# Attention and bilinear FFN on one core: a written order on all engines, six-token loads for batches 0 and 1, and later q transposed by DMA

## The chip, the cores and the metric

One core of a Trainium2 chip runs the whole program in one launch. The metric is the device time of one execution in microseconds; lower is better.

## The reference

Eight batches, eight heads, 576 tokens, head size 64; all inputs are float32. The result has 4608 tokens of 512 values.

```python
kv  = einsum('bhsd,bhse->bhde', k, v)                 # per head 64 x 64, sum over 576 tokens
out = einsum('bhsd,bhde->bhse', q, kv)
x   = out / sqrt(mean(out*out, axis=-1) + 1e-6) * g_norm   # then heads side by side: 4608 x 512
a, b = x @ w_a, x @ w_b                               # 512 -> 1536 each
y   = (a * b) @ w_out                                 # 1536 -> 512
```

## The kernel before

**Attention of one batch** (class `Attn`) goes by head pairs p = 0 to 3, two heads to 128 partitions. `kv(p)` sums over the 576 tokens in five chunks (four of 128 tokens, one of 64) with k as the weights, and ScalarE copies the two diagonal blocks to `kvd` (lines 146 to 162). `qT(p)` transposes q by five TensorE transposes into PSUM, and VectorE copies it to `qs` (164 to 176). `xu(p, h)` multiplies by `kvd` for half of the tokens (288) and ScalarE squares the result; `ss(p, h)` sums the squares by a matmul with a constant matrix, ScalarE takes the reciprocal root, VectorE scales into `xt[p]` (178 to 205). `slices()` yields after each of these pieces: 17 pieces to a batch.

**Loads** (`load_b`, lines 73 to 94) are DMAs from the GpSimd queue that cast float32 to bfloat16. A partition holds four consecutive tokens of a head, a run of 1024 bytes in DRAM and 512 bytes in SBUF; the last 64 tokens go in a second DMA in runs of 256 and 128 bytes. Since TensorE wants the two heads of a pair side by side, VectorE copies k and q into another order first (`reorder`, 125 to 130). The token order inside a batch is thus permuted, and `store` (246 to 264) writes rows with a stride of four to undo it.

**FFN** goes by nine strips of 512 tokens. `ffn_ab(s, fc)` is one of twelve units of a strip: four matmuls with `w_a`, four with `w_b`, each of 512 columns; ScalarE copies the first result, VectorE multiplies the second by it. `ffn_o(s, g)` is twelve matmuls for 128 tokens, a copy and one or two stores from the SP queue.

**Order.** Loads are issued as batch 0, `w_a` and `w_b` in twelve DMAs, batch 1, `w_out` in two, batch 2, then one batch per strip. The program is written as: attention 0, the units of strip 0, attention 1, then strips 1 to 8, where each unit of strip s is followed by a piece of the attention of batch s+1, and every third unit by an `ffn_o` of strip s-1. A planner of the tile framework reorders the instructions within each engine's queue by what it estimates to be ready; `kr` copies of batch 2 can so stand ahead of VectorE work of strip 0. Each engine then runs its queue in order.

Of the kernel before, what the change touches and what calls it, by code (L numbers as in the profile page):

```python
# [8 lines left out]
FP32 = mybir.dt.float32  # L9
# [6 lines left out]
def kernel(  # L16
# [20 lines left out]
    NCH = S // 128  # L37
    SA = NCH * 128
    SB = S - SA
# [24 lines left out]
    def load_ab(i):  # L64
        sl = slice(i * WCH, (i + 1) * WCH)
        nc.gpsimd.dma_start(out=wa_t[:, :, sl], in_=wa_v[:, :, sl])  # L66
        nc.gpsimd.dma_start(out=wb_t[:, :, sl], in_=wb_v[:, :, sl])  # L67

    def load_o(i, n):
        sl = slice(i * n, (i + 1) * n)  # L70
        nc.gpsimd.dma_start(out=wo_t[:, sl, :], in_=wo_v[:, sl, :])

    def load_b(b, parts):
        tiles = {}
        for name in ("k", "v", "q"):
            tiles[name] = qkv_pool.tile([128, H, NCH + 1, D], BF16, name=name + "t", tag=name)
            if name != "v":
                tiles[name + "r"] = qkv_pool.tile(
                    [128, NCH + 1, H, D], BF16, name=name + "r", tag=name + "r", bufs=2
                )  # L80
        hn = H // parts
        for i in range(parts):
            hs = slice(i * hn, (i + 1) * hn)
            for name, src in (("k", k), ("v", v), ("q", q)):
                t = tiles[name]
                nc.gpsimd.dma_start(  # L86
                    out=t[:, hs, 0:NCH, :],
                    in_=src[b, hs, 0:SA, :].rearrange("h (sp c) d -> sp h c d", c=NCH),
                )
# [12 lines left out]
    g_col = const.tile([128, 1], FP32)
    g_src = g_norm.rearrange("(d u) -> d u", u=1)
    nc.sync.dma_start(out=g_col[0:D, :], in_=g_src)
    nc.sync.dma_start(out=g_col[D : 2 * D, :], in_=g_src)
    eps_t = const.tile([128, 1], FP32)
    nc.vector.memset(eps_t, EPS)
    warm = const.tile([128, 1], FP32)
    nc.scalar.activation(warm, eps_t, AF.Abs_reciprocal_sqrt)
    ones = const.tile([128, 128], BF16)  # L110
# [3 lines left out]
    kvd = []  # L114
    for i in range(2):
        t = const.tile([128, NP, 128], BF16, name=f"kvd{i}")
        nc.vector.memset(t, 0.0)
        kvd.append(t)

    xt = []  # L120
    for kc in range(KC):
        xt.append(xt_pool.tile([128, n_tok], BF16, name=f"xt{kc}", tag=f"xt{kc}"))


    def reorder(t, name, hs):
        nc.vector.tensor_copy(
            t[name + "r"][:, 0:NCH, hs, :],
            t[name][:, hs, 0:NCH, :].rearrange("p h c d -> p c h d"),
        )
        nc.vector.tensor_copy(t[name + "r"][0:SB, NCH, hs, :], t[name][0:SB, hs, NCH, :])  # L130

    class Attn:
        def __init__(self, b, t, parts):
            self.b, self.t, self.parts = b, t, parts
            self.kvd = kvd[b % 2]
            self.qs = {}
            self.kv_ps = None
            self.x_ps = {}
            self.sq = {}

        def need(self, name, p):
            n = NP // self.parts
            if p % n == 0:
                reorder(self.t, name, slice(2 * p, 2 * p + 2 * n))

        def kv(self, p):
            if p == 0:
                self.kv_ps = apsum.tile([128, NP, 128], FP32, name="kv_ps", tag="at")
            kt, vt = self.t["kr"], self.t["v"]
            hs = slice(2 * p, 2 * p + 2)  # L150
            self.need("k", p)
            for c in range(NCH + 1):
                r = 128 if c < NCH else SB
                nc.tensor.matmul(  # L154
                    self.kv_ps[:, p, :],
                    lhsT=kt[0:r, c, hs, :],
                    rhs=vt[0:r, hs, c, :],
                    start=(c == 0),
                    stop=(c == NCH),
                )  # L160
            nc.scalar.copy(self.kvd[0:D, p, 0:D], self.kv_ps[0:D, p, 0:D])
            nc.scalar.copy(self.kvd[D:, p, D:], self.kv_ps[D:, p, D:])

        def qT(self, p):
            qt = self.t["qr"]
            hs = slice(2 * p, 2 * p + 2)
            self.need("q", p)
            ps = apsum.tile([128, S], BF16, name="q_ps", tag="at")
            for c in range(NCH + 1):
                r = 128 if c < NCH else SB  # L170
                nc.tensor.transpose(  # L171
                    ps[:, c * 128 : c * 128 + r], qt[0:r, c, hs, :], ident[0:r, 0:r]
                )
            qs = asb_pool.tile([128, S], BF16, name="qs", tag="qs", bufs=5)
            nc.vector.tensor_copy(qs, ps)
            self.qs[p] = qs

        def xu(self, p, h):
            ps = apsum.tile([128, HF], FP32, name="x_ps", tag="at")
            nc.tensor.matmul(  # L180
                ps,
                lhsT=self.kvd[:, p, :],
                rhs=self.qs[p][:, h * HF : (h + 1) * HF],
                start=True,
                stop=True,
            )
            sq = asb_pool.tile([128, HF], BF16, name="sq", tag="sq")
            nc.scalar.activation(sq, ps, AF.Square)  # L188
            self.x_ps[p, h] = ps
            self.sq[p, h] = sq  # L190

        def ss(self, p, h):
            ps = apsum.tile([128, HF], FP32, name="s_ps", tag="at")
            nc.tensor.matmul(ps, lhsT=ones, rhs=self.sq[p, h], start=True, stop=True)  # L194
            rs = asb_pool.tile([128, HF], FP32, name="rs", tag="rs")
            nc.scalar.activation(rs, ps, AF.Abs_reciprocal_sqrt, bias=eps_t)  # L196
            t0 = self.b * S + h * HF
            nc.vector.scalar_tensor_tensor(  # L198
                out=xt[p][:, t0 : t0 + HF],
                in0=self.x_ps[p, h],  # L200
                scalar=g_col,
                in1=rs,
                op0=ALU.mult,
                op1=ALU.mult,
            )

        def slices(self):
            for p in range(NP):
                self.kv(p)
                yield  # L210
                self.qT(p)
                yield
            prev = None
            for p in range(NP):
                for h in range(2):
                    self.xu(p, h)
                    if prev is not None:
                        self.ss(*prev)
                    prev = (p, h)
                    yield  # L220
            self.ss(*prev)
            yield


    ab = {}

    def ffn_ab(s, fc):
        t0 = s * STRIP
        a_ps = fpsum.tile([128, STRIP], FP32, name="a_ps", tag="f")
        b_ps = fpsum.tile([128, STRIP], FP32, name="b_ps", tag="f")  # L230
        for w, ps in ((wa_t, a_ps), (wb_t, b_ps)):
# [117 lines left out]
```

## Time and profile before

| | |
|---|---|
| time, two runs | 369.06 and 369.86 us, median 369.46 us |
| span of the profiled execution | 369.4 us (the profile gives no other time of its own) |
| TensorE busy | 341.7 us, 93% of the span, 1744 matmuls |
| VectorE, ScalarE busy | 149.7 us, 140.2 us |
| GpSimd queue's DMAs | 45,728 packets, 18.88 MB written |
| SP queue's DMAs | 5,664 packets, 9.44 MB written |

Busy time of TensorE is modelled and pipelined, so a busy engine is not one at its peak: the distance between the starts of consecutive matmuls says more. The table's 93% is a mean over a start, in which data is loaded, and a long regular part; the stretches are to be read one by one. MB and GB/s of the loads count the bfloat16 bytes written; the float32 bytes read are twice as many.

### The profile page before, as it was taken

The page shows a single profiled execution, that of the slowest core. Times are in us where ns is not written, and L with a number is a line of the kernel's source. Part 1 is how long each engine was busy: PE and PEld are TensorE (multiplying, and loading weights), DVE is VectorE, ACT ScalarE, POOL GpSimd, SP SyncE. Part 2 cuts the span into 40 slices and gives each one's busy share as a digit, 9 for nine tenths or more (in the row PEclk, how much of TensorE's full clock was granted, in tenths as well). Part 3 has the DMA queues.
Part 4 walks back from the last instruction along what each step waited for, and adds up shares of the span by engine and source line. Part 5 has one row for each costly group of instructions (what it writes and reads, how often), then busy time and mean ns, then how long its engine had stood idle before and what let it go on. Part 6 is the DMA issues. An engine that isn't in the chain of part 4 may idle for free.

```text
span 369.4 us, 4627 instructions
## 1 busy us (share of the span) xinstructions
PE 341.7 (93%) x1744; PEld 163.8 (44%) x1744; DVE 149.7 (41%) x268; ACT 140.2 (38%) x320; POOL 57.6 (16%) x80
## 2 busy tenths in 40 slices
PE   0588859999999999999999999999999999999994
PEld 0333324444444444445444444444444444444441
DVE  1343535545543554355434543354335432222310
ACT  1164113633562356235523552355235522132210
POOL 7955635535000200020000000000000000000000
PEclk9999885699999999999999999999999999999998
DMA  8999999999901511151001111100001111101023
GB/s 96 177 196 192 165 193 192 191 191 204 210 32 30 69 51 31 29 73 49 28 30 28 28 30 29 30 28 29 30 28 30 28 28 30 29 28 59 28 58 85
DMA packets 51414, 28.61 MB, mean 77 GB/s; under 512 B 14528, under 2 KB 46784, under 8 KB 51392
## 3 DMA queue, kind: packets, MB, share of 16 engines
q0 software_dynamic: 45728, 18.88, 41.5%
q1 hardware_dynamic: 5664, 9.44, 9.2%
q8 instruction: 13, 0.21, 0.3%
q14 instruction: 9, 0.07, 0.1%
HBM read 37.75 MB, written 9.44 MB: 128 GB/s over the span
## 4 chain that ended last, share of the span: by engine, by line
PE 81%; DMA 11%; POOL 3%; ACT 2%; DVE 1%; issue 1%; POOLq 0%; ACTq 0%; DVEq 0%
PE o_ps L269 26%; PE a_ps L233 23%; PE b_ps L233 22%; DMA kt<-in_k_dram 4%; PE kv_ps L154 3%; PE q_ps L171 3%; DMA wa_t<-in_moe_w_a_dram 3%; DMA qt<-in_q_dram 2%; PE s_ps L194 2%; DMA vt<-in_v_dram 2%; PE x_ps L180 2%; POOL wb_t L67 1%; POOL wa_t L66 1%; ACT rs L196 1%; ACT sq L188 0%
## 5 line engine op out<-in xcount | busy, mean ns | idle before, releaser
L243 DVE TENSOR_TENSOR abt<-b_ps,a_sb 128x512 bf16<-128x512 f32 x108 | 74.4, 691 | 100.7 <-PE b_ps L233 94.2
L241 ACT CAST a_sb<-a_ps 128x512 bf16<-128x512 f32 x108 | 63.1, 586 | 108.1 <-PE a_ps L233 106.5
L269 PE MATMUL o_ps<-wo_t,abt 128*128 128x512 bf16 x432 | 98.6, 379 | 0.0
L233 PEld LDWEIGHTS <-wb_t 128*128 128x128 bf16 x432 | 42.8, 99 | 60.6 <-issue 13.3
L269 PEld LDWEIGHTS <-abt 128*128 128x128 bf16 x432 | 41.3, 98 | 46.7
L233 PEld LDWEIGHTS <-wa_t 128*128 128x128 bf16 x432 | 39.9, 99 | 39.0 <-issue 2.4
L233 PE MATMUL b_ps<-xt_122,wb_t 128*128 128x512 bf16 x108 | 42.4, 393 | 6.4 <-DVE abt L243 6.4
L233 PE MATMUL a_ps<-xt_122,wa_t 128*128 128x512 bf16 x108 | 42.6, 394 | 0.0
L233 PE MATMUL a_ps<-xt_123,wa_t 128*128 128x512 bf16 x108 | 41.9, 388 | 0.0
L233 PE MATMUL a_ps<-xt_125,wa_t 128*128 128x512 bf16 x108 | 41.2, 381 | 0.7 <-DVE xt_125 L198 0.5
L233 PE MATMUL b_ps<-xt_123,wb_t 128*128 128x512 bf16 x108 | 41.8, 387 | 0.0
L233 PE MATMUL b_ps<-xt_125,wb_t 128*128 128x512 bf16 x108 | 41.4, 384 | 0.0
L233 PE MATMUL b_ps<-xt_124,wb_t 128*128 128x512 bf16 x108 | 41.4, 384 | 0.0
L233 PE MATMUL a_ps<-xt_124,wa_t 128*128 128x512 bf16 x108 | 41.2, 381 | 0.2 <-DVE xt_124 L198 0.2
L188 ACT ACTIVATE sq<-x_ps 128x288 bf16<-128x288 f32 x64 | 26.1, 411 | 33.2 <-PE x_ps L180 32.8
L196 ACT ACTIVATE rs<-s_ps,eps_t 128x288 f32<-128x288 f32 x64 | 31.7, 498 | 1.9 <-PE s_ps L194 1.7
L154 PE MATMUL kv_ps<-vt,kr 128*128 128x128 bf16 (+1 forms) x160 | 20.2, 241 | 13.0 <-DMA vt<-in_v_dram 12.0
L280 DVE COPY o_sb<-o_ps 128x512 f32<-128x512 f32 x18 | 12.5, 692 | 38.3 <-PE o_ps L269 38.3
L278 ACT COPY o_sb<-o_ps 128x512 f32<-128x512 f32 x18 | 10.5, 586 | 45.4 <-PE o_ps L269 45.4
L154 PEld LDWEIGHTS <-kr 128*128 128x128 bf16 (+1 forms) x160 | 13.9, 105 | 24.4 <-issue 6.9
L86 POOL DMA_DIRECT2D vt<-in_v_dram x10 | 9.4, 941 | 77.1 <-PE kv_ps L154 71.6
L194 PE MATMUL s_ps<-sq,ones 128*128 128x288 bf16 x64 | 19.7, 308 | 1.8 <-ACT rs L196 0.7
(42 smaller groups left out, 196.4 us busy)
## 6 DMA issues: line engine op xcount, KB each, us to landing
out_dram<-o_sb SPq DMA_DIRECT2D x40, 128.0 KB, 2.4
out_dram<-o_sb SPq DMA_DIRECT2D x16, 256.0 KB, 2.2
kt<-in_k_dram POOLq DMA_DIRECT2D x6, 512.0 KB, 12.6
vt<-in_v_dram POOLq DMA_DIRECT2D x6, 512.0 KB, 10.7
qt<-in_q_dram POOLq DMA_DIRECT2D x6, 512.0 KB, 12.4
wa_t<-in_moe_w_a_dram POOLq DMA_DIRECT2D x6, 256.0 KB, 8.4
wb_t<-in_moe_w_b_dram POOLq DMA_DIRECT2D x6, 256.0 KB, 9.0
wo_t<-in_moe_w_out_dram POOLq DMA_DIRECT2D x2, 768.0 KB, 9.7
```

Source lines behind the costliest of these rows:

```text
L86: nc.gpsimd.dma_start(out=t[:, hs, 0:NCH, :], in_=src[b, hs, 0:SA, :].rearrange("h (sp c) d -> sp h c d", c=NCH),)
L154: nc.tensor.matmul(self.kv_ps[:, p, :], lhsT=kt[0:r, c, hs, :], rhs=vt[0:r, hs, c, :], start=(c == 0), stop=(c == NCH),)
L171: nc.tensor.transpose(ps[:, c * 128 : c * 128 + r], qt[0:r, c, hs, :], ident[0:r, 0:r])
L188: nc.scalar.activation(sq, ps, AF.Square)
L194: nc.tensor.matmul(ps, lhsT=ones, rhs=self.sq[p, h], start=True, stop=True)
L196: nc.scalar.activation(rs, ps, AF.Abs_reciprocal_sqrt, bias=eps_t)
L233: nc.tensor.matmul(ps, lhsT=w[:, kc, fc * 128 : (fc + 1) * 128], rhs=xt[kc][:, t0 : t0 + STRIP], start=(kc == 0), stop=(kc == KC - 1),)
L241: nc.scalar.copy(a_sb, a_ps)
L243: nc.vector.tensor_mul(t, b_ps, a_sb)
L269: nc.tensor.matmul(o_ps, lhsT=ab[s, fc][:, g * 128 : (g + 1) * 128], rhs=wo_t[:, fc, :], start=(fc == 0), stop=(fc == FC - 1),)
L278: nc.scalar.copy(o_sb, o_ps)
L280: nc.vector.tensor_copy(o_sb, o_ps)
```

## The change

The tile framework's planner is switched off (`manual_schedule`), and every engine runs its instructions as written. PSUM banks and SBUF buffers are assigned by hand. For batches 0 and 1 a partition holds six consecutive tokens of a head (96 partitions, runs of 1536 and 768 bytes), loaded by head pair; k, v and q are used where they lie, one head at a time with 64 columns, and the permuted token order is kept until the stores. For batches 2 to 7 k and v come in natural token order in ten DMAs (runs of 256 and 128 bytes), q goes to a DRAM scratch as bfloat16 with the heads side by side and from there through one transposing DMA on the SP queue into `qT`. The VectorE reorder copies are gone, and for batches 2 to 7 the TensorE transposes with them. For batches 0 and 1 the square, the root and the scaling take 576 columns at once. Matmuls on zeros (`dummy`) are added to batch 0. The four `ffn_o` of strip 0 are moved from strip 1 to between the pieces of attention 1. The last `ffn_o` is stored in two halves.

```diff
-    def reorder(t, name, hs):
...
+    ctx.enter_context(tc.manual_schedule())
+    def load_early(b, p, names="kvq"):
+        hs = slice(2 * p, 2 * p + 2)
+        for n, t, src in (("k", ek, k), ("v", ev, v), ("q", eq, q)):
+            if n in names:
+                nc.gpsimd.dma_start(
+                    out=t[b][:, hs, :, :],
+                    in_=src[b, hs].rearrange("h (t c) d -> t h c d", c=EC),
                 )
...
+    def load_late(b):
+        nc.gpsimd.dma_start(
+            out=qs_d[b - 2].rearrange("t (h d) -> h t d", d=D), in_=q[b]
+        )
+        for t, src in ((lk, k), (lv, v)):
+            for c in range(NCH):
                 nc.gpsimd.dma_start(
+                    out=t[b % 3][:, c, :, :],
+                    in_=src[b, :, c * 128 : (c + 1) * 128, :].rearrange("h p d -> p h d"),
                 )
+            nc.gpsimd.dma_start(
+                out=t[b % 3][0:SB, NCH, :, :],
+                in_=src[b, :, SA:S, :].rearrange("h p d -> p h d"),
+            )
+    def transpose_q(b):
+        nc.sync.dma_start_transpose(qT[b % 2], qs_d[b - 2])
...
+            if self.early:
+                for c in range(EC):
+                    for j in range(2):
+                        r = slice(j * D, (j + 1) * D)
+                        nc.tensor.matmul(
+                            o[r, r],
+                            lhsT=ek[self.b][:, 2 * p + j, c, :],
+                            rhs=ev[self.b][:, 2 * p + j, c, :],
...
+        def qt(self, p, bank):
+            for c in range(EC):
+                for j in range(2):
+                    nc.tensor.transpose(
+                        t[j * D : (j + 1) * D, c, :],
+                        eq[self.b][:, 2 * p + j, c, :],
+                        ident[0:EP, 0:EP],
+                    )
+            nc.vector.tensor_copy(qT[self.b % 2][:, p, :], bank.bitcast(BF16)[:, 0:S])
...
+        def x2(self, p, i0):
+            for h in range(2):
+                nc.tensor.matmul(
+                    P[:, i0 + h, 0:HF],
+                    lhsT=self.kvd[:, p, :],
+                    rhs=qT[self.b % 2][:, p, h * HF : (h + 1) * HF],
...
+            nc.scalar.activation(sq2[p % 2], P[:, i0 : i0 + 2, 0:HF], AF.Square)
...
+    load_early(0, 0)
...
+    make_identity(nc, ident)
...
+    load_early(0, 1)
+    load_early(0, 2)
+    load_early(0, 3)
+    WC = 256
+    for i in range(d_ff // WC):
+        load_ab(i * WC, (i + 1) * WC)
+    for i in range(FC):
+        load_o(i)
+    for p in range(NP):
+        load_early(1, p)
+    for b in range(2, 5):
+        load_late(b)
...
+    dummy(30, f_ps[0])
+    for p in range(NP):
+        A.kv(p, o_ps)
+        A.kv_out(o_ps, p, p + 1)
+        A.qt(p, t_ps[0])
+        if p:
+            A.s2(p - 1, 2, 6)
+        dummy(4, f_ps[0])
+        A.x2(p, 6)
+        dummy(4, f_ps[0])
...
+    ffn_o(0, 0)
+    A.kv(0, kb)
+    A.kv_out(kb, 0, 1)
+    A.qt(0, t_ps[0])
+    for p, g, bank in ((1, 1, o_ps), (2, 2, f_ps[1]), (3, 3, o_ps)):
+        o_mm(0, g, bank, range(0, FC // 2))
+        A.x2(p - 1, 6)
+        A.kv(p, kb)
+        A.kv_out(kb, p, p + 1)
+        A.qt(p, t_ps[0])
+        o_mm(0, g, bank, range(FC // 2, FC))
+        o_out(0, g, bank)
+        A.s2(p - 1, 2, 6)
+    transpose_q(2)
...
+    for s in range(1, N_STRIP):
+        gen = slices(Attn(s + 1)) if s + 1 < B else iter(())
         for fc in range(FC):
...
+            if s > 1 or fc > 1:
+                ffn_ab(s, fc)
+            next(gen, None)
+            if fc % 3 == 2:
+                if s > 1:
+                    ffn_o(s - 1, fc // 3)
+                    next(gen, None)
+            if fc == 6 and s + 2 < B:
+                transpose_q(s + 2)
         for _ in gen:
             pass
+        if s + 4 < B:
+            load_late(s + 4)
```

`kv` and `qt` with `self.early` are those of batches 0 and 1. `s2(p)` follows the pattern of `x2(p)`: two matmuls with `ones`, one root and one scaling of 2 x 288 columns. In strip 1 the first pass of the loop issues units 0 and 1 with `x2(3)` and `s2(3)` of batch 1 between their matmuls. The pieces of `slices` in the changed kernel are four `kv`, one `kv_out` for all pairs, then eight steps of x (one matmul) and s of the step before, and a last s: 14 in all. x uses two PSUM banks in turn, s a third, `kv` the same as s. `dummy(n)` is n matmuls of 128 columns on zeros.

## Rows read from the trace of the kernel before

**Rows 1.** The page: span, and GB/s in 40 slices of 9.24 us.
```profile
span 369.4 us, 4627 instructions
...
GB/s 96 177 196 192 165 193 192 191 191 204 210 32 30 69 51 31 29 73 49 28 30 28 28 30 29 30 28 29 30 28 30 28 28 30 29 28 59 28 58 85
```

**Rows 2.** Stretches: length, each engine's busy time (instructions), clock, DMA share, GB/s.
```profile
22.59:56.70 34.11, 26.94 (x107) 11.39 (x106) 13.28 (x27) 11.06 (x22) 17.76 (x24) 0.90 1.41 185
56.70:74.16 17.46, 15.97 (x84) 8.00 (x82) 9.78 (x20) 9.87 (x28) 9.56 (x12) 0.61 1.58 192
...
106.40:143.30 36.90, 36.90 (x203) 18.20 (x200) 17.30 (x30) 16.30 (x39) 1.88 (x2) 1.00 0.25 46
...
254.40:291.50 37.10, 37.04 (x203) 18.19 (x201) 15.34 (x26) 16.16 (x39) 0.00 (x0) 1.00 0.09 29
...
320.48:351.56 31.08, 31.08 (x145) 14.07 (x144) 9.69 (x14) 8.20 (x14) 0.00 (x0) 1.00 0.09 35
```

**Rows 3.** Waits in 0 to 75 us: who for whom, total us, times, longest.
```profile
DVE kr L126 <- DMA kt<-in_k_dram: 12.8, 4, 6.2
...
PE b_ps L233 <- DVE abt L243: 6.4, 2, 4.2
```

**Rows 4.** Timeline, VectorE: start, length, instruction, idle time before and its releaser.
```profile
15.47 0.43 DVE L126 COPY qr<-qt 128x1024 bf16<-128x1024 bf16 x1 [2.37 <-DMA qt<-in_q_dram]
...
53.30 0.69 DVE L126 COPY kr<-kt 128x2048 bf16<-128x2048 bf16 x1 [6.21 <-DMA kt<-in_k_dram]
```

**Rows 5.** Timeline, TensorE in strip 3: starts and lengths of groups.
```profile
147.40 0.52 PE L171 MATMUL q_ps<-ident,qr 128*128 128x128 bf16 x5
147.85 0.39 PE L233 MATMUL a_ps<-xt_122,wa_t 128*128 128x512 bf16 x1
...
149.59 0.55 PE L154 MATMUL kv_ps<-vt,kr 128*128 128x128 bf16 x5
150.07 2.76 PE L269 MATMUL o_ps<-wo_t,abt 128*128 128x512 bf16 x12
...
166.38 0.29 PE L180 MATMUL x_ps<-qs,kvd_118 128*128 128x288 bf16 x1
166.50 0.29 PE L194 MATMUL s_ps<-sq,ones 128*128 128x288 bf16 x1
```

**Rows 6.** Page and table by shape: mean ns of ScalarE and VectorE operations.
```profile
L241 ACT CAST a_sb<-a_ps 128x512 bf16<-128x512 f32 x108 | 63.1, 586 | 108.1 <-PE a_ps L233 106.5
L196 ACT ACTIVATE rs<-s_ps,eps_t 128x288 f32<-128x288 f32 x64 | 31.7, 498 | 1.9 <-PE s_ps L194 1.7
...
L243 DVE TENSOR_TENSOR abt<-b_ps,a_sb 128x512 bf16<-128x512 f32 x108 | 74.4, 691 | 100.7 <-PE b_ps L233 94.2 <-ACT a_sb L241 2.4 <-PE a_ps L233 2.3
...
L198 DVE SCALAR_TENSOR_TENSOR xt_122<-x_ps,g_col,rs 128x288 bf16<-128x288 f32 x16 | 8.3, 518 | 5.2 <-ACT rs L196 5.2
```

**Rows 7.** Timeline, TensorE around a pause: matmuls of the same shape.
```profile
38.41 0.38 PE L233 MATMUL b_ps<-xt_122,wb_t 128*128 128x512 bf16 x1 [2.17 <-DVE abt L243]
...
40.21 0.63 PE L233 MATMUL a_ps<-xt_125,wa_t 128*128 128x512 bf16 x1
40.64 0.63 PE L233 MATMUL b_ps<-xt_122,wb_t 128*128 128x512 bf16 x1
```

**Rows 8.** Timeline, GpSimd: issues of weights' and batches' DMAs, and what each waited for.
```profile
18.68 0.75 POOL L67 DMA_DIRECT2D wb_t<-in_moe_w_b_dram  x1 [0.25 <-DMA wb_t<-in_moe_w_b_dram]
...
32.02 0.62 POOL L90 DMA_DIRECT2D kt<-in_k_dram  x1 [0.58 <-DMA wb_t<-in_moe_w_b_dram]
...
56.81 0.88 POOL L86 DMA_DIRECT2D qt<-in_q_dram  x1 [1.45 <-DMA vt<-in_v_dram]
...
75.45 0.88 POOL L86 DMA_DIRECT2D kt<-in_k_dram  x1 [1.52 <-DVE abt L243]
```

**Rows 9.** The page's queues: packets, MB, share of 16 engines' span.
```profile
q1 hardware_dynamic: 5664, 9.44, 9.2%
```

**Rows 10.** Timeline of the end: last matmuls, last copy, last store's issue.
```profile
351.39 13.11 PE L269 MATMUL o_ps<-wo_t,abt 128*128 128x512 bf16 x60
...
364.59 0.59 ACT L278 COPY o_sb<-o_ps 128x512 f32<-128x512 f32 x1 [4.64 <-PE o_ps L269]
...
365.71 0.60 SPq L261 DMA_DIRECT2D out_dram<-o_sb  x1
```

More of the change, by code (lines that the diff above doesn't have):

```diff
@@ L36 @@
     NP = H // 2
-    NCH = S // 128
-    SA = NCH * 128
-    SB = S - SA
     HF = S // 2
@@ new lines, with ab_begin, ab_mm, ab_out_a @@
+    n_ab = [0]
+    def ab_begin():
+        i = n_ab[0]
+        n_ab[0] += 1
+        return f_ps[(2 * i) % 4], f_ps[(2 * i + 1) % 4], a_sb[i % 4]
+    def ab_mm(s, fc, bank, w, kcs):
+        t0 = s * STRIP
+        for kc in kcs:
+            nc.tensor.matmul(
+                bank,
+                lhsT=w[:, kc, fc * 128 : (fc + 1) * 128],
+                rhs=xt[kc][:, t0 : t0 + STRIP],
+                start=(kc == 0),
+                stop=(kc == KC - 1),
+            )
+    def ab_out_a(a, t):
+        nc.scalar.copy(t, a)
@@ new lines, with o_mm, o_out @@
+    n_o = [0]
+    def o_mm(s, g, bank, fcs, e0=0, e1=d_model):
+        for fc in fcs:
+            nc.tensor.matmul(
+                bank[:, e0:e1],
+                lhsT=abt[s % 2][fc][:, g * 128 : (g + 1) * 128],
+                rhs=wo_t[:, fc, e0:e1],
+                start=(fc == 0),
+                stop=(fc == FC - 1),
+            )
+    def o_out(s, g, bank):
+        i = n_o[0]
+        n_o[0] += 1
+        t = o_sb[i % 4]
+        if i % 2:
+            nc.scalar.copy(t, bank)
+        else:
+            nc.vector.tensor_copy(t, bank)
+        store(s * STRIP + g * 128, t, 0, d_model)
@@ L103, with ffn_o, dummy @@
+    def ffn_o(s, g, bank=None):
+        bank = bank or o_ps
+        o_mm(s, g, bank, range(FC))
+        o_out(s, g, bank)
+    def dummy(n, bank):
+        for _ in range(n):
+            nc.tensor.matmul(bank[:, 0:128], lhsT=zeros, rhs=zeros, start=True, stop=True)
     g_src = g_norm.rearrange("(d u) -> d u", u=1)
+    nc.vector.memset(zeros, 0.0)
+    load_early(0, 0)
     nc.sync.dma_start(out=g_col[0:D, :], in_=g_src)
     nc.sync.dma_start(out=g_col[D : 2 * D, :], in_=g_src)
-    eps_t = const.tile([128, 1], FP32)
@@ L132 @@
[L132 to L221, printed above, removed]
-            yield
@@ new lines, with slices @@
+    transpose_q(2)
+    def slices(A):
+        kb = t_ps[0]
+        for p in range(NP):
+            A.kv(p, kb)
+            yield
+        A.kv_out(kb, 0, NP)
+        yield
+        prev = None
+        for i in range(2 * NP):
+            A.x(i // 2, i % 2, t_ps[1 + i % 2])
+            if prev is not None:
+                A.s(prev // 2, prev % 2, t_ps[0], t_ps[1 + prev % 2])
+            prev = i
+            yield
+        A.s(prev // 2, prev % 2, t_ps[0], t_ps[1 + prev % 2])
+        yield
@@ L317 @@
-    for g in range(STRIP // 128):
-        ffn_o(N_STRIP - 1, g)
+        if s + 4 < B:
+            load_late(s + 4)
+    last = N_STRIP - 1
+    for g in range(3):
+        ffn_o(last, g, (o_ps, t_ps[0])[g % 2])
+    hw = d_model // 2
+    r0 = last * STRIP + 3 * 128
+    o_mm(last, 3, f_ps[0], range(FC), 0, hw)
+    nc.vector.tensor_copy(o_sb[3][:, 0:hw], f_ps[0][:, 0:hw])
+    store(r0, o_sb[3], 0, hw)
+    o_mm(last, 3, f_ps[1], range(FC), hw, d_model)
+    nc.scalar.copy(o_sb[3][:, hw:], f_ps[1][:, hw:])
```

315 lines of the change are left out of this document (177 added, 138 removed).

## Prediction

> **What bounds the kernel now.** I read the page's slices first, then the busy time by stretch, then the waits of the start, then the timeline of TensorE. The loads keep the DMA engines at about 190 GB/s for the first 100 us and then fall to about 30 [rows 1]: the kernel has a start, and a regular part. In the regular part TensorE is the bound and has no idle time: five strips between 106.40 and 291.50 us take 36.9 to 37.1 us each, and a strip without attention takes 31.08 us for 144 matmuls of 512 columns [rows 2], 0.216 us apiece. So attention costs 37.0 - 31.1 = 5.9 us a strip, and only fewer TensorE columns make this part shorter. The start is different: of 34.1 us from 22.59 to 56.70 TensorE is busy 26.9, with 107 matmuls, and from 56.70 to 74.16 the granted clock averages 0.61 [rows 2]. The cause is in the waits: VectorE stood 12.8 us waiting for k of a batch to copy, and its FFN products behind those copies held TensorE's b matmuls for 6.4 us [rows 3]. One such copy, of batch 2, began at 53.30 after 6.21 us of waiting [rows 4], while strip 0 was unfinished.
>
> **The path after, in five terms.** The sum is made on the profiled execution's span, 369.4 us [rows 1]; the two runs' median lies 0.06 us above it.
>
> *Steady strips.* The five transposes of a pair hold TensorE from 147.40 to 147.85, 0.45 us; kv from 149.59 to 150.07, 0.48; x and s of 288 columns 0.12 each [rows 5]. Four times 0.48, four times 0.45 and 16 times 0.12 make 5.6 of the 5.9. The transposes go: 4 x 0.45 = 1.8 us a strip, 9.0 us for strips 2 to 6. VectorE's reorder copies and q copies go too, but VectorE was busy 15 to 17 of 37 us [rows 2]: worth nothing here. The written order keeps two banks for x. Step i waits for the scaling of step i-2: 0.29 us of s, 0.4 of the other square ahead of it on ScalarE, 0.50 root and 0.52 scaling [rows 5, 6], 1.7 us against steps of 8 x 0.216 + 0.12 = 1.85 us. It just fits; I charge nothing, at most 0.3 us for each of 8 steps, 2.4 a strip.
>
> *Strip 0.* Batch 0 was complete at about 15.5 [rows 4]. In pair pieces the same 1.77 MB at 192 GB/s [rows 2] needs 9.2 us after some 3 us of first issue, so I put the last pair at 13 (12 to 15.5). A pair's chain: 12 small kv matmuls and 12 small transposes, half as wide as those of rows 5, each between half and all of 0.096 and 0.090 us: 1.1 to 2.2 us, taken as 1.5; below that if the two heads overlap in the array. x and s 0.5. Root and scaling of 576 columns, between once and twice 498 and 518 ns, with the 512-wide rows at 586 and 691 [rows 6]: 0.72 and 0.74. Dummies and hops 0.45. That is 3.9 us a pair at full clock, because scaling p-1 must leave the x banks before x of p. From a first pair at 5 us, the last x2 comes at 19 us. At the lower of TensorE's two levels, 1.2 GHz, a 512-column matmul takes 0.43 instead of 0.216 us (starts 40.21 to 40.64, after a pause of 2.17 us [rows 7]); with TensorE's terms doubled a pair takes 6.1 us and the last x2 comes at 27. Twelve prepared matmuls cover the last scaling (2.6 us), then 4 x 0.216 + 10 units x 1.73 = 18.2 us remain. Strip 0 ends at 40 at full clock throughout, 48 at the lower clock until about 25 us; I take 44, since work as scattered as this gets the lower clock at 57 to 74 us [rows 2]. The dummies are there to raise it earlier, which no row can price.
>
> *Attention 1 and the four output groups.* 4 x 12 x 0.216 = 10.4 us; batch 1's attention 4 x 1.5 + 16 x 0.12 = 7.9, of which 0.5 falls into strip 1; waits for x banks 1.0. Strip 1 starts at 44 + 18.8 = 62.8. Cover: everything up to batch 1 is the 8.26 MB that had landed in the old kernel at 53.3 - 3.1 = 50.2 us (the batch-2 k landed at 53.30 [rows 4], one k takes 3.1 us, below). So w_out and batch 1 arrive ahead of their use.
>
> *Strip 1.* 12 units 20.7, the rest of batch 1 0.5, kv 1.9, x and s 1.9. Eleven calls serve 14 pieces, so x6, s6, x7, s7 stand without cover: 3.6 us by the waits above (2 to 5). Strip 2 starts at 62.8 + 28.6 = 91.4 instead of 106.4: 15.0 us earlier. From there 5 x (37.0 - 1.8) and the unchanged strips 7 and 8.
>
> *End.* The last matmul ends at 364.5, its copy takes 0.59, and two store issues follow, the second at 365.71 [rows 10]. Half a copy and one issue of 0.6 less: 0.6 us gained, 0 to 1.
>
> Sum: 369.4 - 15.0 - 9.0 - 0.6 = **344.8 us**, 345 rounded.
>
> **The late loads**, which I cost at nothing because strips 1 to 6 cover them. Batches 2 to 7 come in 576 x 8 pieces of 128 written bytes for each of k, v and q: 13,824 pieces, 864 on each of 16 engines. The trace has their like, the last 64 tokens of each tensor. The weights' DMAs, 32 pieces of 512 bytes per engine, followed each other at (32.02 - 18.68)/10 = 1.33 us; a tensor of 64 such pieces and 32 short ones at (75.45 - 56.81)/6 = 3.11 us [rows 8]. So 41.7 ns for a long piece and (3.11 - 64 x 0.0417)/32 = 13.7 ns for a short one, and 864 x 13.7 ns = 11.8 us a batch. Batch 2 lands at 62; its kv is due two units into strip 1, at 67. Each later batch has 35 us. GpSimd issues 11 DMAs a batch, under 1 us each [rows 8]; nothing else waits on that queue.
> The q scratch is written in DRAM, which no row shows for short pieces. The nearest row is the stores: 9.2% x 16 x 369.4 / 5,664 = 96 ns for 2 KB [rows 9]. Between 13.7 and 96 I take the first, whose pieces have the same size.
> The Trainium skill, DMA: Bandwidth & Descriptors, section Specifications, says that below 512 bytes the DMA engine does a read-modify-write. Rows 8 do not show it for writes into SBUF; the rule would make the sum that of the first rival.
> The transposing DMA has no row either. SP issues it behind strip 0's last store, at 63; x of batch 2 is due five units and four kv after 67, at 77.6. So up to 15 us cost nothing, later ones have 29; 0.59 MB at 192 GB/s would be 3.1. Stores queue behind it on SP, with four output buffers at one per 8.7 us.
>
> **Rivals.**
> *Short pieces at double price, 27.4 ns.* 23.7 us a batch: batch 2 lands at 73.9, 6.9 us late, and batch 3 in time: 352. If q's leading dimension of 8 also keeps it on 8 engines, (576 + 576) x 27.4 = 31.6 us a batch: 14.8 late, then 5.3 more: 365. For it: the DRAM side is unseen. Against: rows 8. Chance 0.18.
> The Trainium skill, same page, section Why a DMA increments its semaphore by 16 and not by 1, lets the slowest dimension set the number of engines; no row here shows such a DMA.
> *Slower: the late loads set the pace.* A batch comes at P, the seventh lands at 50.2 + 6P, and behind it 33.5 us of strip 6, 73.0 of the rest and 4.3 of the end remain. From P = 36 the time is 377 and above. That is the price if a short piece costs as much as one of 512 bytes (864 x 41.7 ns = 36.0); with q's pieces at 96 ns on 16 engines P is 7.9 + 27.6 = 35.5, on 8 engines 63 and the time 539. Against: rows 8 again. Chance 0.06.
> *The written order stalls.* The 1.85 us step fails by 0.3 us in all 48 steps (14 us) and the clock stays low to the end of attention 1 (10 us more): 369. Against: the old order had the same two-step distance and rows 5 show no gap. Chance 0.06.
> *More gain.* Heads overlapping in the array halve the small matmuls (3 us in strip 0, 4 in batch 1), and full clock gives 4 more: 334 and below. Chance 0.06 below 333.
>
> **Numbers.** The forecast (333 to 352) has 0.64. Predicted 345, range 333 to 361: below lies 0.06, above the rest of the first rival (0.05) and the two bad ones. A measurement tells 2%, 7.4 us, from no change: faster means below 362. Faster 0.64 + 0.06 + 0.16 = 0.86; same 0.08; slower 0.06.
>
> **What would show it.** After: strip 2's first unit near 91 us; strips 2 to 6 at 35.2 us; no VectorE wait for k; kv of batch 2 without a DMA wait. A TensorE wait on `lk`, `lv` or `qT` in strip 1 shows the first rival, the same in every strip the second. I am wrong if strip 0 ends after 48, if strips 2 to 6 take over 36 us, or if the q scratch takes over 10 us.

## The result, and the profile after

The changed kernel took 351.75 us (351.20 to 352.31) against 369.46: ratio 0.952, 95% interval 0.948 to 0.957. Predicted were 345 and a range of 333 to 361. The profiled execution took 352.31, with a span of 350.5. Here and below, executions that took over 1.5% longer than the fastest of the same kernel are left out of the times and ratios.

I read the same views as before. The page first: the span and the 40 slices, now of 8.76 us (GB/s, answering [rows 1]), with the busy share of TensorE and its granted clock, then the queues [rows 9].

```profile
span 350.5 us, 4664 instructions
...
PE   6689998599599999999999999999999999999995
...
PEclk9559999999989999999999999999999999999999
...
GB/s 96 180 196 201 177 141 135 192 103 137 106 145 91 168 140 143 128 131 154 50 32 97 31 32 30 97 32 31 32 30 30 32 30 31 55 36 30 33 60 90
...
q0 software_dynamic: 124704, 18.99, 71.5%
q1 hardware_dynamic: 19696, 12.98, 16.4%
```

The loads now run until about 160 us, and after the first 45 us most slices show 90 to 170 GB/s where they had shown 190. TensorE dips in the slices from 61 and 88 us, both in strip 1. The busy time by stretch [rows 2] cuts the run at strip 0's units, attention 1, the strips, and the end:

```profile
22.84:44.91 22.07, 22.04 (x100) 9.85 (x99) 8.33 (x12) 8.12 (x14) 13.91 (x24) 0.96 1.30 189
44.91:61.04 16.13, 14.89 (x158) 7.61 (x156) 5.45 (x9) 5.27 (x15) 10.22 (x10) 1.00 1.48 135
61.04:95.87 34.83, 26.30 (x139) 12.57 (x136) 13.09 (x21) 16.14 (x33) 21.51 (x21) 1.00 1.98 136
95.87:132.88 37.01, 36.67 (x181) 17.26 (x180) 14.62 (x24) 15.05 (x32) 22.78 (x22) 0.95 1.89 133
132.88:168.09 35.21, 35.21 (x182) 16.91 (x180) 13.73 (x22) 15.02 (x32) 13.83 (x14) 1.00 1.89 140
...
238.50:273.70 35.20, 35.20 (x182) 16.99 (x181) 13.73 (x22) 15.20 (x33) 0.00 (x0) 1.00 0.09 30
273.70:304.80 31.10, 31.10 (x146) 14.09 (x145) 9.68 (x14) 8.21 (x15) 0.00 (x0) 1.00 0.09 35
```

Strip 2 starts at 95.87 instead of 106.40: 10.5 us. Strips 2 to 6 take 177.8 instead of 185.1: 7.3. From there to the end it is 76.8 instead of 77.9: 1.1. Together 18.9, the difference of the two spans. The forecast's 15.0, 9.0 and 0.6 made 24.6; strip 1 holds most of the gap. Its waits, in TensorE's timeline (start, length, instruction, idle time before and its releaser):

```profile
63.12 0.38 PE L251 MATMUL P<-xt,wa_t 128*128 128x512 bf16 x1 [1.49 <-DVE xt L204]
...
66.63 0.38 PE L251 MATMUL P<-xt,wa_t 128*128 128x512 bf16 x1 [0.45 <-DVE xt L204]
...
69.70 0.22 PE L155 MATMUL P<-lv,lk 128*128 128x128 bf16 x1 [1.88 <-DMA lv<-in_v_dram]
70.95 0.21 PE L155 MATMUL P<-lv,lk 64*128 64x128 bf16 x1 [1.03 <-DMA lv<-in_v_dram]
...
92.73 0.28 PE L215 MATMUL P<-qT,kvd 128*128 128x288 bf16 x1 [1.38 <-DVE xt L231]
...
94.51 0.28 PE L215 MATMUL P<-qT,kvd 128*128 128x288 bf16 x1 [1.38 <-DVE xt L231]
...
95.75 0.28 PE L226 MATMUL P<-sq,ones 128*128 128x288 bf16 x1 [0.83 <-ACT rs L227]
...
97.17 0.58 PE L251 MATMUL P<-xt,wa_t 128*128 128x512 bf16 x1 [0.34 <-DVE xt L231]
97.55 1.91 PE L251 MATMUL P<-xt,wb_t 128*128 128x512 bf16 x4
...
99.98 0.39 PE L251 MATMUL P<-xt,wa_t 128*128 128x512 bf16 x1
```

Three kinds stand here: batch 1's last scaled pieces (1.49 and 0.45), v of batch 2 (1.88 and 1.03), and the pieces of batch 2 left over after the units (x6, s5, x7, s6 and s7, from 91.06 to 95.87). Behind the last the clock falls: four matmuls take 1.71 us from 97.55 to 99.26, 0.43 apiece and so 1.2 GHz, where 0.216 is usual. GpSimd's issues and waits [rows 8] show what v waited for:

```profile
45.29 2.97 POOL L113 DMA_DIRECT2D qs<-in_q_dram  x1 [1.19 <-issue]
59.57 0.88 POOL L118 DMA_DIRECT2D lv<-in_v_dram  x1 [5.32 <-DMA qs<-in_q_dram]
62.72 2.97 POOL L113 DMA_DIRECT2D qs<-in_q_dram  x1 [0.50 <-DMA lk<-in_k_dram]
...
140.98 2.97 POOL L113 DMA_DIRECT2D qs<-in_q_dram  x1 [0.74 <-DMA lk<-in_k_dram]
```

Five batches lie between the first and the last issue of a q scratch, so a batch takes (140.98 - 45.29)/5 = 19.1 us; 11.8 were predicted. In the page's DMA issues (count, KB, median us from issue to landing) the q scratch is the slowest, and k queued behind it is nearly as slow:

```profile
qs<-in_q_dram POOLq DMA_DIRECT2D x6, 576.0 KB, 15.4
lk<-in_k_dram POOLq DMA_DIRECT2D x24, 128.0 KB, 14.1
```

### The profile page after: what moved, and what is told of

The parts are those of the page before. It is cut to its first block, busy times and chain, and to the rows that moved or that the text cites. A ratio compares the mean times of both kernels' runs of the same rounds, so it can differ in the third digit from the quotient of the medians.

```text
span 350.5 us, 4664 instructions
## 1 busy us (share of the span) xinstructions
PE 328.0 (94%) x1810; PEld 160.3 (46%) x1810; DVE 122.8 (35%) x198; ACT 130.4 (37%) x268; POOL 99.5 (28%) x120
## 4 chain that ended last, share of the span: by engine, by line
PE 77%; DMA 15%; POOL 3%; issue 2%; ACT 1%; DVE 0%; ACTq 0%; POOLq 0%
PE P L251 47%; PE P L291 24%; DMA wb_t<-in_moe_w_b_dram 5%; DMA qs<-in_q_dram 4%; DMA lv<-in_v_dram 3%; PE P L155 3%; DMA wo_t<-in_moe_w_out_dram 2%; PE P L215 2%; PE P L226 2%; DMA eq<-in_q_dram 1%; POOL ev L100 1%; POOL ek L100 1%; POOL eq L100 1%; ACT rs L227 1%; POOL lv L118 0%
## 5 line engine op out<-in xcount | busy, mean ns | idle before, releaser
L263 DVE TENSOR_TENSOR ab<-P,asb 128x512 bf16<-128x512 f32 x108 | 74.5, 691 | 127.0 <-PE P L251 123.6
L251 PE MATMUL P<-xt,wa_t 128*128 128x512 bf16 x432 | 113.1, 382 | 2.3 <-DVE xt L204 1.9
L251 PE MATMUL P<-xt,wb_t 128*128 128x512 bf16 x432 | 112.5, 381 | 0.0
L260 ACT CAST asb<-P 128x512 bf16<-128x512 f32 x108 | 63.1, 586 | 110.9 <-PE P L251 109.1
L291 PE MATMUL P<-wo_t,ab 128*128 128x512 bf16 (+1 forms) x444 | 99.2, 373 | 0.9 <-ACT osb L304 0.7
L291 PEld LDWEIGHTS <-ab 128*128 128x128 bf16 x444 | 42.8, 98 | 47.3 <-issue 1.1
L231 DVE SCALAR_TENSOR_TENSOR xt<-P,g_col,rs 128x288 bf16<-128x288 f32 x48 | 24.8, 517 | 25.8 <-ACT rs L227 25.8
L118 POOL DMA_DIRECT2D lv<-in_v_dram x24 | 21.2, 897 | 40.1 <-DMA qs<-in_q_dram 36.9
L227 ACT ACTIVATE rs<-P,eps_t 128x288 f32<-128x288 f32 x48 | 23.8, 496 | 2.4 <-PE P L226 2.4
L118 POOL DMA_DIRECT2D lk<-in_k_dram x24 | 21.3, 915 | 0.0
L215 PE MATMUL P<-qT,kvd 128*128 128x288 bf16 x48 | 13.7, 285 | 2.8 <-DVE xt L231 2.8
L155 PEld LDWEIGHTS <-lk 128*128 128x128 bf16 (+1 forms) x120 | 9.8, 98 | 10.6 <-issue 2.7
L226 PE MATMUL P<-sq,ones 128*128 128x288 bf16 x48 | 13.7, 286 | 0.8 <-ACT rs L227 0.8
## 6 DMA issues: line engine op xcount, KB each, us to landing
qs<-in_q_dram POOLq DMA_DIRECT2D x6, 576.0 KB, 15.4
```

The source lines that it names most:

```text
L118: nc.gpsimd.dma_start(out=t[b % 3][:, c, :, :], in_=src[b, :, c * 128 : (c + 1) * 128, :].rearrange("h p d -> p h d"),)
L155: nc.tensor.matmul(o, lhsT=lk[self.b % 3][0:m, c, hs, :].rearrange("p h d -> p (h d)"), rhs=lv[self.b % 3][0:m, c, hs, :].rearrange("p h d ...
L215: nc.tensor.matmul(bank[:, 0:HF], lhsT=self.kvd[:, p, :], rhs=qT[self.b % 2][:, p, h * HF : (h + 1) * HF], start=True, stop=True,)
L226: nc.tensor.matmul(bank[:, 0:HF], lhsT=ones, rhs=sq[i % 4], start=True, stop=True)
L227: nc.scalar.activation(rs[i % 4], bank[:, 0:HF], AF.Abs_reciprocal_sqrt, bias=eps_t)
L231: nc.vector.scalar_tensor_tensor(out=xt[p][:, t0 : t0 + HF], in0=xbank[:, 0:HF], scalar=g_col, in1=rs[i % 4], op0=ALU.mult, op1=ALU.mult,)
```

## The experiments

My theory: the gain is what the prediction says (the reorder copies gone from the start, TensorE transposes gone from the strips), and the missing 6 us lie in strip 1, in the late loads and in pieces without cover. The rival: the written order itself is the gain. The numbers below are medians; the ratio is against the kernel before, with its interval. The kernels that are not built on before are built on the changed one.

**The changed kernel again**, beside other runs on the same chip:

> The changed kernel again, unaltered, beside the others on the same chip: 350 to 352.5, with a wait for v of batch 2 of 0 to 3 us.

350.34 us, 0.947 (0.944 to 0.951). In this trace v was never waited for. From the first kv of batch 2 to its last are 6.77 us (68.35 to 75.12), in the profile above 9.78: that wait comes and goes between executions and is worth up to 3.0 us.

**The written order alone**, put on the kernel before:

```diff
+    ctx.enter_context(tc.manual_schedule())
     const = ctx.enter_context(tc.tile_pool(name="const", bufs=1))
```

> The old kernel with the planner switched off and nothing else: every engine runs its instructions as written. Theory A, the order alone gave the gain of the start: no copy of batch 2 stands ahead of strip 0's products, the waits of 6.4 us for VectorE go, and the time is 355 to 362. Theory B, the written order needs the other edits (the output groups between the pieces of attention 1, no reorder copies): attention 1 stands uncovered, in every strip TensorE waits some 2 us for the two reorder copies just ahead of their matmuls, and the time is 370 to 385.

393.84 us, 1.065 (1.060 to 1.071): a loss. TensorE's waits (who for whom, total us, times, longest) and two stretches:

```profile
PE kv_ps L155 <- DVE kr L127: 12.1, 9, 1.5
PE q_ps L172 <- DVE qr L127: 9.5, 7, 1.5
```

```profile
49.50:74.78 25.28, 19.34 (x95) 8.12 (x96) 11.82 (x27) 10.76 (x29) 10.34 (x13) 0.73 1.58 192
...
116.44:158.00 41.56, 37.41 (x201) 17.99 (x200) 16.92 (x31) 16.27 (x38) 4.69 (x6) 1.00 0.49 69
```

A strip takes 41.6 us, 4.6 over the planner's 37.0 [rows 2], and TensorE waits up to 1.5 us for a reorder copy that is written just ahead of its use. In the changed kernel these copies are gone, and its strips have no gap. So the rival fails for the whole, but not for strip 0, whose units begin and end here with

```profile
25.59 1.93 PE L234 MATMUL a_ps<-xt,wa_t 128*128 128x512 bf16 x4
...
47.31 1.03 PE L234 MATMUL b_ps<-xt,wb_t 128*128 128x512 bf16 x4
```

They take 22.6 us without a gap, as in the changed kernel (22.07), and end at 48.2, where the planner's order ended them at about 56.5: no copy of batch 2 stands ahead of their products. So most of what strip 0 gained comes with the order, even with the copies left in, as theory A had it for this stretch. By strip 2 it is lost again: its first unit starts at 105.92, before at 106.40. The other edits under the planner were not run, so how the start's gain divides between the order and the loss of the copies stays open.

**Late q by TensorE**: q of batches 2 to 7 loaded like k and v, transposed by TensorE, no scratch and no transposing DMA.

```diff
-        nc.gpsimd.dma_start(
-            out=qs_d[b - 2].rearrange("t (h d) -> h t d", d=D), in_=q[b]
-        )
-        for t, src in ((lk, k), (lv, v)):
+        for t, src in ((lq, q), (lk, k), (lv, v)):
...
+                nc.tensor.transpose(
+                    t[:, c * 128 : c * 128 + m],
+                    lq[(self.b - 2) % 3][0:m, c, hs, :].rearrange("p h d -> p (h d)"),
+                    ident[0:m, 0:m],
+                )
+            nc.vector.tensor_copy(qT[self.b % 2][:, p, :], t)
```

> Undoes one part: q of batches 2 to 7 is loaded into SBUF in the same short pieces as k and v and transposed by TensorE, five transposes to a pair; no scratch, no transposing DMA. Theory A, the term of the sum: strips 2 to 6 take 37.0 instead of 35.2 us and strip 1 1.8 us more, together 10.8; and short pieces into SBUF cost 13.7 ns, so a late batch comes every 12 us and the 2.9 us wait for v in strip 1 goes; time about 359.5. Theory B, the transposing DMA and the scratch give back by contention what they save: 350 to 354. If short pieces into SBUF cost 20 ns or more, the pace stays above 17 us and the wait stays, 362.

412.96 us, 1.119 (1.114 to 1.124). In this edit two of the `lq` buffers share memory with `eq`, and the late loads stand ahead of batch 0's reads in the program, so batch 0 waits for a later batch's q and is computed with it (its own q is left out):

```profile
PE P L173 <- DMA eq<-in_q_dram: 54.5, 2, 54.1
```

It says nothing of the question. One number of it holds: GpSimd issued three batches of short pieces one behind the other without waiting for any, the second in 12.45 us (56.01 to 68.46), and the DMAs landed 4.4 to 5.0 us (medians) after their issue. So a 128-byte piece into SBUF costs at most 12.45/864 = 14.4 ns; 13.7 was predicted. With the loads moved behind batch 1's reads:

> Undoes one part: q of batches 2 to 7 is loaded into SBUF in the same short pieces as k and v and transposed by TensorE, five transposes to a pair; no scratch, no transposing DMA. Batches 3 and 4 are loaded after batch 1's q is used. Theory A, the term of the sum: strips 2 to 6 take 37.0 us instead of 35.2 and strip 1 1.8 us more, 10.8 us together; short pieces into SBUF cost 13.7 ns, so v of batch 2 lands in time and up to 2.9 us of waiting go: 359 to 363. Theory B, scratch and transposing DMA give back by contention what they save TensorE: strips of 35.2 to 36 us and 351 to 354.

361.22 us, 0.977 (0.974 to 0.980), 10.9 above the changed kernel run beside it. One of its strips:

```profile
108.30:145.26 36.96, 36.96 (x201) 18.18 (x200) 15.57 (x26) 15.15 (x32) 12.58 (x15) 1.00 0.86 77
```

36.96 against 35.20: the transposes are worth 1.76 us a strip, predicted 1.8. Six strips make 10.6 of the 10.9. Without the scratch TensorE waits for no load of batch 2 in this trace.

**The q scratch with tokens outermost:**

```diff
-            out=qs_d[b - 2].rearrange("t (h d) -> h t d", d=D), in_=q[b]
+            out=qs_d[b - 2].rearrange("t (h d) -> t h d", d=D),
+            in_=q[b].rearrange("h t d -> t h d"),
```

> The only edit is the order of dimensions of the q scratch transfer: tokens outermost instead of heads. Theory A, the leading dimension of 8 kept the scratch transfer on half of the DMA engines, so that it and the k and v queued behind it came late: the scratch transfer lands in 8 to 9 us instead of 15, the pace of a late batch falls from 18.6 us to 12 to 14, the 2.9 us in which kv of batch 2 waits for v goes, and the time falls from 351.75 to about 348.5. Theory B, each short write to DRAM is dear, on however many engines: the pace stays between 17 and 20 us, the wait stays at 2 to 3 us, and the time is 351 to 352.

350.36 us, 0.949 (0.947 to 0.951): no different from the changed kernel by time. The trace does differ. A scratch lands 9.3 us after its issue (median) instead of 15.4, and the first and the last of the six go out at

```profile
44.34 2.22 POOL L113 DMA_DIRECT2D qs<-in_q_dram  x1 [1.18 <-issue]
...
114.33 2.31 POOL L113 DMA_DIRECT2D qs<-in_q_dram  x1
```

(114.33 - 44.34)/5 = 14.0 us a batch, and one of these five stretches holds 2.50 us of waiting for a buffer of k. So a leading dimension of 8 had cost at least 5 us a batch. The Trainium skill, DMA: Bandwidth & Descriptors, section Why a DMA increments its semaphore by 16 and not by 1, says that the slowest dimension sets the number of engines; these two landing times agree, though the views do not show how many engines each transfer used. TensorE waits for no v here, as in the repeat of the changed kernel; the leftover pieces of strip 1 still cost 1.38, 1.38 and 0.71.

**Leftover pieces between units**: the last pieces of batch 2 stand between the first three quarters of units 0 and 1 of strip 2.

```diff
+        if s == 1:
+            us = [(f,) + ab_begin() for f in (0, 1)]
+            for kc in range(2):
+                for f, a, b, t in us:
+                    ab_mm(2, f, a, wa_t, [kc])
+                    ab_mm(2, f, b, wb_t, [kc])
+            next(gen)
...
         for _ in gen:
             pass
```

> The last uncovered pieces of batch 2's attention (x6 to s7, at the end of strip 1) are interleaved with the first three quarters of two units of strip 2. Theory A, the uncovered pieces and the lower clock that follows them cost 4 to 6 us: the 3.9 us of TensorE waits there fall to 1.5 or less, the stretch at 1.2 GHz shortens, and the span falls by 2.5 to 4 us. Theory B, the chain of square, root and scaling through two PSUM banks sets the start of strip 2 whatever runs beside it: the waits only move to the fourth quarter of these units and the span stays within 1 us.

349.33 us, 0.945 (0.942 to 0.949), whose interval overlaps that of the changed kernel. In the trace, from the last kv of batch 2 to the last kv of batch 3 are 27.72 us (76.15 to 103.87), against 29.74 and 30.31 in the two runs of the changed kernel: 2.0 to 2.6 gained. Three waits stay, 1.38, 0.83 and 1.14, two of them for the scaling; but behind them the clock keeps its level, and four matmuls take 0.87 us (99.06 to 99.93):

```profile
PEclk9999999999999999999999999999999999999999
```

For the first 27 us this row is no evidence: it shows 9 there, while matmuls of 512 columns start 0.43 us apart (three in 1.28 us, 24.08 to 25.36), which is 1.2 GHz.

**No matmuls on zeros:** `dummy` issues none.

> The matmuls on zeros are left out; nothing else changes. Theory A, they raise the clock early: without them strip 0's first units run at 1.2 GHz for some 3 to 4 us more, strip 0 ends 2 to 3 us later than 44.9 us, and the time is about 354. Theory B, they only stand in the way of the chain of batch 0 (8 of them to a pair, 0.9 us at the lower clock): strip 0 ends 1 us earlier, 350.5.

349.94 us, 0.948 (0.947 to 0.950): no different from the changed kernel. In batch 0, x of one pair follows x of the pair before by 3.9 us (13.28, 17.13, 21.04) instead of 4.3. By the starts of the 512-column matmuls strip 0 runs at 1.2 GHz until 25.8; in the two traces of the changed kernel until 24.6 and until about 27. Its units end at 44.98, there at 44.91 and 45.76. So no gain in the clock is shown for the dummies, and what they cost is no more than what differs between executions.

**k and v of all batches in six-token form** (four DMAs a batch, 64-column kv):

```diff
+        for hs in (slice(0, H // 2), slice(H // 2, H)):
+            for t, src in ((ek, k), (ev, v)):
+                nc.gpsimd.dma_start(
+                    out=t[b % 3][:, hs, :, :],
+                    in_=src[b, hs].rearrange("h (t c) d -> t h c d", c=EC),
+                )
```

> The changed kernel, except that k and v of batches 2 to 7 too come in the six-token form (96 partitions, runs of 1536 and 768 bytes, four DMAs a batch) and kv is 12 matmuls of 64 columns, one head at a time; q as before by scratch and transposing DMA. Theory A, the two heads of a pair overlap in the array: 12 such matmuls hold TensorE for 0.21 us in batch 1, where 5 matmuls of 128 columns hold it for 0.48; strips 1 to 6 lose 4 x 0.27 = 1.1 us each (strips 2 to 6 at 34.1 us), the wait for v goes, and the time is 343 to 345. Theory B, the 0.21 us is an artefact of where the matmuls stood in batch 1 and each costs at least half of a 128-column one: 12 x 0.048 = 0.58 us, strips of 35.6, 351 to 353.

348.51 us, 0.942 (0.937 to 0.947), whose interval overlaps that of the changed kernel. (All k and v now share three buffers each, so the loads of batches 3 and 4 stand later in the program.) A strip takes 34.82, 0.38 less than 35.20: a gain, but a third of theory A's 1.1. Between 512-column matmuls a group of twelve small ones holds TensorE 0.31 us, and 0.09 go ahead of it, together 0.40 where five of 128 columns took 0.48:

```profile
131.78 0.38 PE L251 MATMUL P<-xt,wb_t 128*128 128x512 bf16 x1
132.09 0.38 PE L145 MATMUL P<-ev,ek 96*64 96x64 bf16 x12
132.40 1.04 PE L251 MATMUL P<-xt,wa_t 128*128 128x512 bf16 x4
```

**Several edits together.** `c1` takes the scratch with tokens outermost; two x banks for batch 0 without the dummies between its pieces; a third x bank and one quarter unit more for the leftover pieces; the root of batch 1 three matmuls earlier; and the o banks of the last strip swapped. Two of the five edits:

```diff
-            A.s2(p - 1, 2, 6)
-        dummy(4, f_ps[0])
-        A.x2(p, 6)
-        dummy(4, f_ps[0])
+            A.s2(p - 1, 2, 0 if p % 2 else 6)
+        A.x2(p, 6 if p % 2 else 0)
...
-        o_mm(0, g, bank, range(FC // 2, FC))
-        o_out(0, g, bank)
+        o_mm(0, g, bank, range(FC // 2, FC // 2 + 3))
         A.s2(p - 1, 2, 6)
+        o_mm(0, g, bank, range(FC // 2 + 3, FC))
+        o_out(0, g, bank)
```

> The changed kernel with five edits at the places where TensorE still waits: the scratch transfer with tokens outermost; batch 0's wide x in two pairs of banks in turn, without the dummies between; the root and scaling of batch 1 three matmuls earlier in each output group; a third bank for x of batch 2 and its last pieces between three quarters of two units of strip 2; and the last strip's first output in another bank than the one just before. By my readings: strip 0 ends 3 to 5 us earlier, strip 1 starts another 1 to 2 us earlier, the wait for v (0 to 3 us) goes, strip 2 starts without the 4 us of waits and the 1.5 us of lower clock, the end gains 0.7: time 337 to 342. Rival: the loads then set the start (w_out and batch 1 land at 37 and 49 us, batch 2 at 60), and only half is gained: 344 to 347.

342.55 us, 0.925 (0.920 to 0.930). Strip 0 ends at 40.89, strip 1 starts at 55.68; but v of batch 2 still came after it was needed, and kv waited 1.50, 2.33 and 0.96 us, after which the granted clock was 0.50 from 67.3 to 72.0 us, that is 1.2 GHz. The profiled execution took 345.87, the longest of four; the shortest took 340.18 at a mean granted clock of 0.999, so at least the stretch at 1.2 GHz does not come in every execution.

`c4` is `c1` with k and v in six-token form, and batch 2's scratch issued behind its k and v (only the place of the scratch is shown; `not False` is always true):

```diff
+        if b != 2 or False:
+            load_q(b)
+        for hs in (slice(0, H // 2), slice(H // 2, H)):
...
+        if b == 2 and not False:
+            load_q(b)
```

> The five edits of the earlier combination together with k and v of batches 2 to 7 in the six-token form, and for batch 2 q's scratch behind k and v. From that combination's span of 344.1: 1.1 us less in each of six strips (6.6), the wait for v of 4.8 us gone with the 2.5 us of lower clock behind it: 330 to 333. Rival: x of batch 2 then waits for the transposing DMA, which cannot start before the scratch has landed (about 60 us, then 9 us more, against a need at 71): up to 5 us back, 335 to 338.

344.04 us, 0.931 (0.927 to 0.934), the rival's mechanism at a higher price: now x of batch 2 waited 6.61 us for `qT`. With the scratch first again (`c5`):

```diff
-        if b != 2 or False:
+        if b != 2 or True:
...
-        if b == 2 and not False:
+        if b == 2 and not True:
```

> The kernel that the experiments point to: batch 0's x banks used in turn without the inner matmuls on zeros, the root of batch 1 moved earlier between the output groups, the drain of batch 2 interleaved with units 0 and 1 of strip 2, k and v of all batches in six-token form, the q scratch written with tokens outermost and, for batch 2 too, ahead of k and v. Theory (the late loads of batch 2 were the last wait of strip 1, and q's order only decides which of two operands is late): against c4 the 6.6 us of waiting for qT goes and k, v of batch 2 come 4 to 8 us later, with at most 1 us of waiting for them; strips 2 to 6 keep c4's length; 336 to 339 us, no stretch at 1.2 GHz after 45 us. Rival (the loads of batch 2 are late in either order, since the early strips now end 5 us sooner): kv of batch 2 waits 3 us or more for ev, and a stretch at 1.2 GHz follows; 341 to 344 us.

343.01 us, 0.927 (0.923 to 0.932). The rival came in its time, but not in its place: k and v were in time, and `qT` still came 4.91 us late, with a clock of 0.81 from 77 to 92. The transposing DMA went out at 57.8 and landed 19.2 us later, while GpSimd's queue filled the DMA engines with batches 3 and 4.

```profile
77.03 0.40 PE L216 MATMUL P<-qT,kvd 128*128 128x288 bf16 x1 [4.91 <-DMA qT<-qs]
```

`c6` holds those loads back: one k and one v buffer for all late batches, and from batch 3 on q behind them. Part of the edit against `c5` (the early calls for batches 3 and 4 are gone as well):

```diff
-                    out=t[b % 3][:, hs, :, :],
+                    out=t[0][:, hs, :, :],
...
             if fc == 6 and s + 2 < B:
+                load_late(s + 2)
                 transpose_q(s + 2)
...
-        if s + 4 < B:
-            load_late(s + 4)
```

> The kernel c5 with the loads of batches 3 to 7 held back: k and v of every late batch share one buffer, so the loads of a batch are issued only when kv of the batch before it has been computed, and its q scratch goes behind its k and v. Batch 2's loads stay as in c5. In c5 the transposing DMA of batch 2 took 19.2 us from its issue at 57.8 to its landing at 77.0, while the DMA engines were filled with loads of batches 3 and 4. Theory (it was late by sharing the engines with those loads): with nothing else to move between 55 and 67 us it lands within 8 us, x of batch 2 waits less than 0.5 us for qT, no stretch at 1.2 GHz follows in strip 1; 336 to 339 us. Rival (the transposing DMA is slow by itself, or q's scratch lands late): x of batch 2 still waits 3 us or more for qT; 341 to 344 us. Rival (the hold makes the later batches late): a wait for ev or qT in strips 2 to 6, 1 us or more in each; 344 us and above.

**336.80 us, 0.910 (0.906 to 0.914)**, the fastest kernel here. Its page's clock, GpSimd's issues around the hold, and the transposing DMAs (us from issue to landing, least, median, most; then the same line of `c5`):

```profile
PEclk9569999999999999999999999999999999999999
```

```profile
48.05 1.19 POOL L121 DMA_DIRECT2D ev<-in_v_dram  x1
64.62 0.68 POOL L121 DMA_DIRECT2D ek<-in_k_dram  x1 [15.38 <-PE P L146]
```

```profile
DMA to landing us min/median/max: 4.6/4.8/5.9
```

```profile
DMA to landing us min/median/max: 4.6/9.1/19.2
```

Between 49 and 64 us no load is issued, the transposed q lands in time, x of batch 2 waits for nothing, and the clock stays up after strip 0's start. Batch 2's scratch is issued at 44.34 us and its transposing DMA at 57.83, in `c5` at 44.23 and 57.80; what differs between them is what else was moving. This confirms that the transposing DMA was late beside those loads: here none took over 5.9 us. Loading a batch as early as possible had cost 6 us.

## Why the prediction was right, and where it was off

*Steady strips: right.* Predicted 35.2 us a strip; strips 3 to 6 took 35.20 to 35.21 with no gap, and TensorE's transposes put back gave 36.96. The written order's step of 1.85 us fits, as charged. Strip 2 alone took 37.0, which was not foreseen: some 1.8 us more, for the last wait on the leftover pieces (0.34) and the clock that fell behind them.

*Strip 0: right in its mechanism, in its size partly by luck.* Predicted to end at 44, ended at 44.91. The pair chain is as described: between x of one pair and x of the next stand 4.3 us, with 1.26 of waiting for the scaling that must leave the x banks:

```profile
13.35 0.64 PE L182 MATMUL P<-qT,kvd 128*128 128x288 bf16 x2 [1.26 <-DVE xt L204]
...
17.63 0.64 PE L182 MATMUL P<-qT,kvd 128*128 128x288 bf16 x2 [1.26 <-DVE xt L204]
```

But 44 was put between 3.9 us a pair at full clock and 6.1 at the lower. The chain ran at 1.2 GHz (the two x matmuls hold TensorE 0.43 us, 13.35 to 13.78, where 0.12 each is usual), and the last x started at 21.98, not at 27: twelve kv and twelve transposes, 3.0 us in that case, took 0.94 (14.35 to 15.29). A clock worse than the middle and matmuls cheaper than priced cancel. With two bank pairs (`c6`, which also leaves out the dummies between) x starts at 11.59, 13.92 and 16.14, 2.3 us apart; without the dummies alone they were 3.9 apart. This confirms the banks as the limit.

*Attention 1: too high by 2.7 us* (16.1 against 18.8). The term mis-sized is the small matmuls, priced at 1.5 us a pair from the half-width rows:

```profile
50.08 0.38 PE L145 MATMUL P<-ev,ek 96*64 96x64 bf16 x12
50.29 0.43 PE L172 MATMUL P<-ident,eq 96*64 96x96 bf16 x12
50.65 1.47 PE L291 MATMUL P<-wo_t,ab 128*128 128x512 bf16 x6
```

Twelve kv take 0.21 us and twelve transposes 0.36: 0.57 a pair, with 0.1 ahead of them, below the lower bound of 1.1; an overlap of the heads had been named as what would bring it below. Strip 1 started at 61.04 instead of 62.8.

*Strip 1: the step that failed*, 34.8 instead of 28.6. Three terms: batch 1's last scaled pieces (1.9 us of waits, not priced); leftover pieces without cover (4.8 instead of 3.6, and five pieces, not the four that were named); and the late loads, costed at nothing (2.9 in this trace, none in the repeat). A late batch came every 19.1 us, not every 11.8, and the wait on `lv` is the sign that was named for the first rival. That rival's 352 fits the measured time, but its mechanism is 2.9 of strip 1's 6.2. Two of the named signs of being wrong came: a scratch took over 10 us (15.4), and strip 2 over 36. The short pieces into SBUF fit the predicted price (at most 14.4 ns against 13.7), but the scratch did not, and with tokens outermost 14.0 us a batch were measured: I took the SBUF price for writes in DRAM, and dropped the eight-engine case into a rival. The Trainium skill, DMA: Bandwidth & Descriptors, section Specifications, names a read-modify-write below 512 bytes; for writes into SBUF no run shows one. The transposing DMA, up to 15 us free, took 11.8 in the median and was no wait here, only later, when strip 1 had come sooner.

*End: right in size.* From strip 7 on 1.1 us less, predicted 0.6, although TensorE waited 0.67 us for an o bank.

The sum, in spans: 345 - 1.8 (start of strip 1) + 6.2 (strip 1) + 1.8 (strip 2) - 0.5 (end) gives 350.7; 350.5 was measured.

## What to carry to other kernels

A load that is cheap on its own queue is not cheap for the transfer beside it: price a prefetch by what it takes from the one transfer that is due next, and hold it back by a buffer. When a layout change removes on-chip copies, look at the one strip where start and steady state meet: loads, banks and uncovered last pieces all come due there. A written order pays only where no engine is asked for a result just written; test it alone.

## What the runs showed of the hardware

- Two heads' 64-column matmuls in different column halves overlap: twelve, 768 columns, in 0.21 us, where one of 512 columns takes 0.216 and five of 128 columns 0.48 [rows 5]. Between 512-column matmuls twelve cost 0.40 (`e_kv6`).
- One transposing DMA of 576 x 512 bfloat16 took at most 5.9 us with the loads held back (`c6`) and up to 19.2 us beside them (`c5`).
- TensorE fell to 1.2 GHz behind a single wait of 4.91 us (`c5`), behind 4.8 us of waits in three parts (`c1`, its longest execution) and behind 3.6 us in three parts with only 288-column matmuls between them (the changed kernel), but not behind 3.35 us in three parts with 512-column matmuls between them (`e_drain`), nor behind v's 2.9 us in two parts.
